# Attention with a rotation and mixing layer: an order from a longest-chain plan, weights turned by DMA, fp16 mixing halves

## The chip, the cores and the metric

One core of one Trainium2 chip. The metric is the device time of one execution in microseconds (us), lower is better. The kernel runs on TensorE (PE in the profile, PEld for its weight loads), VectorE (DVE), ScalarE (ACT), GpSimd (POOL) and SyncE (SP), whose queue issues all the DMAs here.

## What is computed

Eight batches of eight heads of causal attention over 576 positions with a window of 128 and a slope per head, then a layer over the 512 channels of each batch. Cut to what matters:

```python
scores = q @ k.T / sqrt(64) - slope[h] * (t - s)        # where 0 <= t - s < 128, else -1e9
attn = softmax(scores);  x[b] = concat over heads of attn @ v   # 576 x 512
theta = x @ w_theta
zr, zi = x * cos(theta), x * sin(theta)
y = w_tok_r @ zr + w_tok_i @ zi                         # mixes the 576 positions
u = x + y
out = u + maximum(u @ w_ch, 0)
```

The weights come in as 64-bit floats, whose words the kernel takes apart itself. All products are made from two halves of each operand (a high part and the rest), in three products out of four.

## The kernel before, in words

Work is done by pairs of heads (32 pairs, four to a batch). For a pair, q and k are loaded (L176, L178) and split into halves on ACT, DVE and POOL (L230 to L234). `Pair.scores` multiplies them (L289: six products a tile and pair of heads, five tiles), DVE adds the mask and takes the minimum of each row (L296), and ACT makes the exponentials (L300). `Head.turned` turns the weights on PE, nine transposes a head, into a PSUM tile `t_ps` (L320). Batch 0 ("early" heads) copies that out in fp32 (L356). From batch 1 on ("late" heads) `flip` writes two fp16 halves from PSUM into `pt`: the high one on ACT (L366), the low one on DVE (L367). `values` multiplies them with fp16 halves of v (L337: 27 matmuls a late head), and `finish` divides (L343 to L346) into `x_sb`, of which there is one buffer.

When a batch is whole, `turn` transposes x (L390), splits it (L401, L402), multiplies with w_theta (L410: 12 matmuls of 512 columns a column block), makes sine and cosine (L421 to L432; they need another table of ACT than the exponentials, hence the ACT_TABLE_LOADs) and writes z = x cos, x sin as two fp32r halves `z_hi`, `z_lo` (L434 to L440, L381 on ACT, L382 on POOL). `mix` is the big product with the token weights: 8 groups of 27 matmuls of 288 columns a batch, all operands fp32r (L469), then u and its halves (L474 to L476). `channels` is 8 groups of 12 matmuls (L489), a DVE step (L492) and the store (L494).

The order: Python generators interleave the mixing of batch b with the attention of batch b+1 (`attend`), and the channels of b with the turn of b+1 (`rotated`); priorities (MIX, CHAN, ROTATE) are hints to the language's scheduler, which sets the final order of each engine. While batch 0's attention runs, `unpack` takes the weights apart in 17 jobs (L127 to L150), mostly on DVE and POOL.

Of the kernel before, what the change touches and what calls it, by code (L numbers as in the profile page):

```python
# [11 lines left out]
F32 = mybir.dt.float32  # L12
# [4 lines left out]
BF16 = mybir.dt.bfloat16  # L17
# [26 lines left out]


@with_exitstack
def attn_moe_kernel(ctx: ExitStack, tc: tile.TileContext, qt, kt, vx, wth, wtok, wch, band, out):
    nc = tc.nc
    PSUM = bass.MemoryType.PSUM

    const = ctx.enter_context(tc.tile_pool(name="const", bufs=1))
    ld = ctx.enter_context(tc.tile_pool(name="ld", bufs=1))
    qk = ctx.enter_context(tc.tile_pool(name="qk", bufs=1))
    vp = ctx.enter_context(tc.tile_pool(name="vp", bufs=2))
    vbp = ctx.enter_context(tc.tile_pool(name="vbp", bufs=2))
    sp = ctx.enter_context(tc.tile_pool(name="sp", bufs=6))
    ptp = ctx.enter_context(tc.tile_pool(name="ptp", bufs=4))
    xp = ctx.enter_context(tc.tile_pool(name="xp", bufs=1))
    xtp = ctx.enter_context(tc.tile_pool(name="xtp", bufs=2))
    tp = ctx.enter_context(tc.tile_pool(name="tp", bufs=2))  # L60
    uf = ctx.enter_context(tc.tile_pool(name="uf", bufs=2))
    big = ctx.enter_context(tc.tile_pool(name="big", bufs=1))
    ps_s = ctx.enter_context(tc.tile_pool(name="ps_s", bufs=1, space=PSUM))
    ps_t = ctx.enter_context(tc.tile_pool(name="ps_t", bufs=2, space=PSUM))
    ps_a = ctx.enter_context(tc.tile_pool(name="ps_a", bufs=1, space=PSUM))
    ps_m = ctx.enter_context(tc.tile_pool(name="ps_m", bufs=3, space=PSUM))

    class Ring:


        def __init__(self, at, width, count):
            self.at, self.width, self.count, self.n = at, width, count, 0

        def take(self):
            c = self.at + self.n % self.count * self.width
            self.n += 1
            return fixed[:, c:c + self.width]

# [12 lines left out]
    nc.sync.dma_start(out=bnd, in_=band)
    nc.vector.memset(ones, 1.0)

    for g in range(H // 2):
        for e in range(2):
            nc.vector.memset(scales[64 * e:64 * e + 64, g:g + 1], -0.125 * 2.0 ** (2 * g + e + 1))

    wth_hi = const.tile([128, 4, DM], F32R, name="wth_hi")
    wth_lo = const.tile([128, 4, DM], F32R, name="wth_lo")
    wch_hi = const.tile([128, 4, DM], F32R, name="wch_hi")  # L100
    wch_lo = const.tile([128, 4, DM], F32R, name="wch_lo")
    wtk_hi = const.tile([128, 9, S], F32R, name="wtk_hi")
    wtk_lo = const.tile([128, 9, S], F32R, name="wtk_lo")

    nc.vector.memset(rebias, -float(916 << 23))

    ORDER = (0, 4, 1, 5, 2, 6, 3, 7, 8)

    def unpack(jobs, places):

        def load(k):
            src, hi, lo, c, w, scale = jobs[k]
            pool, name = places[k % len(places)]
            t = pool.tile([128, 4 * S], I32, name=name)
            nc.sync.dma_start(out=t[:, :2 * w], in_=src[:, c, :].bitcast(I32))
            return t

        def words(k, t):  # L120
            w = jobs[k][4]
            raw = t[:, :2 * w].rearrange("p (n t) -> p n t", t=2)
            return raw, t[:, 2 * S:2 * S + w], t[:, 3 * S:3 * S + w]

        def apart(k, t):
            raw, ex, ma = words(k, t)
            nc.vector.tensor_scalar(out=ex, in0=raw[:, :, 1], scalar1=0x7FF00000, scalar2=None,  # L127
                                    op0=ALU.bitwise_and)
            nc.vector.tensor_scalar(out=ma, in0=raw[:, :, 1], scalar1=0xFFFFF, scalar2=0x100000,
                                    op0=ALU.bitwise_and, op1=ALU.bitwise_or)  # L130
            nc.scalar.activation(ex, ex, AF.Relu, bias=rebias, scale=8.0)

        def together(k, t):
            raw, ex, ma = words(k, t)
            val = ma.bitcast(F32)
            nc.vector.scalar_tensor_tensor(out=ex, in0=raw[:, :, 1], scalar=-0x80000000, in1=ex,
                                           op0=ALU.bitwise_and, op1=ALU.bitwise_or)
            nc.vector.scalar_tensor_tensor(out=val, in0=raw[:, :, 0].bitcast(U32), scalar=2.0 ** -32, in1=ma,
                                           op0=ALU.mult, op1=ALU.add)
            nc.gpsimd.tensor_tensor(out=val, in0=val, in1=ex.bitcast(F32), op=ALU.mult)  # L140

        def split(k, t):
            _, hi, lo, c, w, scale = jobs[k]
            val = words(k, t)[2].bitcast(F32)
            if scale is None:
                nc.scalar.copy(hi[:, c, :], val)
                nc.gpsimd.tensor_tensor(out=lo[:, c, :], in0=val, in1=hi[:, c, :].bitcast(F32), op=ALU.subtract)
            else:
                nc.scalar.activation(hi[:, c, :], val, AF.Copy, scale=scale)
                nc.vector.scalar_tensor_tensor(out=lo[:, c, :], in0=val, scalar=scale, in1=hi[:, c, :].bitcast(F32),  # L150
                                               op0=ALU.mult, op1=ALU.subtract)

        tiles = {}
        n = len(jobs)
        for k in range(n + 3):
            for stage, fn in ((3, split), (2, together), (1, apart)):
                j = k - stage
                if 0 <= j < n:
                    if j not in tiles:
                        tiles[j] = load(j)  # L160
                    fn(j, tiles[j])
                    if stage == 3:
                        del tiles[j]
                    yield
            if k < n and len(tiles) < len(places):
                tiles[k] = load(k)

    JOBS = ([(wth, wth_hi, wth_lo, c, DM, TURN) for c in range(4)]
            + [(wtok, wtk_hi, wtk_lo, c, S, None) for c in ORDER])
    LATE = [(wch, wch_hi, wch_lo, c, DM, None) for c in range(4)]  # L170


    def load_pair(p):
# [538 lines left out]
```

## Time and profile before

| | |
|---|---|
| time, median of 3 runs | 796.17 us (796.0 to 796.47) |
| span of the profiled execution | 794.3 us, 1.9 us under that median; the page gives no other time for it |
| PE busy / PEld busy | 735.4 us (93%) / 651.7 us (82%) |
| DVE / ACT / POOL busy | 570.5 (72%) / 481.5 (61%) / 259.2 us (33%) |
| moved by DMA | 49.65 MB, mean 62 GB/s |
| clock granted to TensorE | 1.000 throughout |

All numbers below are of core 0, in us from the start of the span. "Busy" of PE is the time covered by matmuls from start to modelled end, so pipelined matmuls cover each other; what a matmul costs is read from the distance of the starts, or from a run of many in the chain of waits. A "DVE busy" of a window is covered time too.

### The profile page before, as it was taken

The numbers are of one execution on the slowest core, as the hardware profiler recorded it, in microseconds if no ns is written. First come the engines' busy times: TensorE is split into PE (matmuls) and PEld (weight loads), VectorE is DVE, ScalarE is ACT, GpSimd is POOL, SyncE is SP. The second block draws the span as 40 slices with busy tenths as digits, with TensorE's granted clock in tenths as the row PEclk, the third lists the DMA queues.
The fourth block names the chain that finished last, engine by engine and source line by source line (L and its number), as shares of the span: only waits on it lengthen the run. The fifth ranks groups of instructions, "written<-read, shape, count | busy, mean of one in ns | idle before, by whom it ended". The sixth has DMA issues, their size and how long they took to land.

```text
span 794.3 us, 16395 instructions
## 1 busy us (share of the span) xinstructions
PE 735.4 (93%) x6338; PEld 651.7 (82%) x6338; DVE 570.5 (72%) x1535; ACT 481.5 (61%) x962; POOL 259.2 (33%) x324
## 2 busy tenths in 40 slices
PE   3655799899999999999999999999999999999998
PEld 2444687789788898989888988999898988899897
DVE  5999847888767887687767777778767776654712
ACT  5445447776477656775668557855677666844610
POOL 3577511532143213332243215321423215210530
PEclk9999999999999999999999999999999999999999
DMA  6453211122202211022212211112102221000001
GB/s 239 153 173 108 65 44 50 31 65 64 84 30 72 65 46 53 24 64 68 80 38 65 65 45 61 52 60 80 53 24 65 65 74 48 2 1 32 31 1 60
DMA packets 29549, 49.65 MB, mean 62 GB/s; under 512 B 2592, under 2 KB 19104, under 8 KB 29472
## 3 DMA queue, kind: packets, MB, share of 16 engines
q1 hardware_dynamic: 29472, 48.61, 19.4%
q8 instruction: 50, 0.82, 0.4%
q14 instruction: 27, 0.22, 0.1%
HBM read 39.16 MB, written 9.44 MB: 61 GB/s over the span
## 4 chain that ended last, share of the span: by engine, by line
PE 62%; DVE 15%; ACT 15%; issue 4%; DMA 2%; POOL 1%; SPq 0%; DVEq 0%; ACTq 0%; POOLq 0%
PE mm L469 20%; PE mm L489 10%; PE t_ps L320 8%; PE mm L410 8%; PE s_ps L289 7%; PE acc L337 7%; ACT s_sb L300 6%; DVE f L425 2%; ACT g L431 2%; ACT z_hi L381 2%; DVE s_sb L296 2%; PE mm L390 2%; DVE g L427 1%; ACT L300 1%; ACT L431 1%
## 5 line engine op out<-in xcount | busy, mean ns | idle before, releaser
L469 PE MATMUL mm<-wtk_hi,z_hi 128*128 128x288 f32 x576 | 172.1, 304 | 3.0 <-ACT z_hi L381 1.7
L469 PE MATMUL mm<-wtk_lo,z_hi 128*128 128x288 f32 x576 | 171.2, 301 | 0.0
L469 PE MATMUL mm<-wtk_hi,z_lo 128*128 128x288 f32 x576 | 166.3, 299 | 0.5 <-POOL z_lo L382 0.5
L300 ACT ACTIVATE s_sb<-s_sb,fixed 128x256 f32<-128x256 f32 (+2 forms) x320 | 128.3, 465 | 54.6 <-DVE fixed L296 54.6
L296 DVE CUSTOM_DVE_ANT_0 s_sb<-s_ps,fixed 128x256 f32<-128x256 f32 (+2 forms) x320 | 105.3, 374 | 21.4 <-PE t_ps L320 11.3
L469 PEld LDWEIGHTS mm<-wtk_hi,z_hi 128*128 128x128 f32 x576 | 107.6, 188 | 6.6 <-ACT z_hi L381 2.1
L320 PE MATMUL t_ps<-fixed,s_sb 128*128 128x128 f32 (+1 forms) x576 | 103.1, 294 | 10.1 <-ACT s_sb L300 9.6
L469 PEld LDWEIGHTS mm<-wtk_lo,z_hi 128*128 128x128 f32 x576 | 108.0, 189 | 1.9
L469 PEld LDWEIGHTS mm<-wtk_hi,z_lo 128*128 128x128 f32 x576 | 106.2, 188 | 1.9 <-POOL z_lo L382 0.7
L476 POOL TENSOR_TENSOR u_lo<-xtf,u_hi 128x288 fp32r<-128x288 f32 x64 | 52.1, 822 | 138.4 <-ACT u_hi L475 125.8
L382 POOL TENSOR_TENSOR z_lo<-g,z_hi 128x512 fp32r<-128x512 f32 x40 | 54.6, 1365 | 126.2 <-ACT z_hi L381 126.2
L367 DVE SCALAR_TENSOR_TENSOR pt<-t_ps,pt 128x512 f16<-128x512 f32 x112 | 74.8, 683 | 23.6 <-ACT pt L366 23.6
L320 PEld LDWEIGHTS t_ps<-fixed,s_sb 128*128 128x128 f32 (+1 forms) x576 | 67.2, 150 | 27.2 <-ACT s_sb L300 14.5
L366 ACT ACTIVATE pt<-t_ps 128x512 f16<-128x512 f32 x112 | 63.5, 594 | 24.8 <-PE t_ps L320 24.3
L289 PE MATMUL s_ps<-kh,qh 64*128 64x256 f32 (+2 forms) x320 | 57.0, 341 | 21.9 <-DVE fixed L296 14.8
L234 POOL TENSOR_TENSOR kl<-kr,kh 128x576 fp32r<-128x576 f32 x32 | 46.6, 1457 | 71.9 <-ACT kh L233 62.4
L337 PE MATMUL acc<-vh,pt 128*128 128x65 f16 x1008 | 61.5, 195 | 2.7 <-DVE pt L367 1.7
L289 PEld LDWEIGHTS s_ps<-kh,qh 64*128 64x128 f32 (+1 forms) x320 | 32.8, 190 | 36.9 <-DVE fixed L296 14.9
L337 PEld LDWEIGHTS <-pt 128*128 128x128 f16 x1512 | 52.7, 98 | 10.0 <-DVE pt L367 2.6
L337 PE MATMUL acc<-vl,pt 128*128 128x64 f16 x504 | 55.9, 193 | 0.0
L475 ACT CAST u_hi<-xtf 128x288 fp32r<-128x288 f32 x64 | 27.2, 429 | 46.6 <-DVE xtf L474 46.6
L289 PE MATMUL s_ps<-kh,ql 64*128 64x256 f32 (+2 forms) x320 | 50.4, 300 | 5.0 <-DVE ql L231 5.0
(115 smaller groups left out, 1568.2 us busy)
## 6 DMA issues: line engine op xcount, KB each, us to landing
vb<-in_vx_dram SPq DMA_DIRECT2D x16, 650.0 KB, 4.3
qr<-in_qt_dram SPq DMA_DIRECT2D x32, 288.0 KB, 3.1
kr<-in_kt_dram SPq DMA_DIRECT2D x32, 288.0 KB, 2.8
out_dram<-xtf SPq DMA_DIRECT2D x64, 144.0 KB, 1.8
xtf<-in_wtok_dram SPq DMA_DIRECT2D x4, 576.0 KB, 4.9
u_hi<-in_wtok_dram SPq DMA_DIRECT2D x3, 576.0 KB, 3.8
u_lo<-in_wtok_dram SPq DMA_DIRECT2D x2, 576.0 KB, 3.9
xtf<-in_wth_dram SPq DMA_DIRECT2D x2, 512.0 KB, 9.4
```

Of the source, the lines that this page charges most:

```text
L289: nc.tensor.matmul(ps[:qn, e, 256 * k:256 * k + kn], qm[rows, q0:q0 + qn], km[rows, k0:k0 + kn], start=(j == 0), stop=(j == len(self.terms ...
L296: nc.vector.tensor_tensor_reduce(out=sb, in0=ps[:qn, e, 256 * k:256 * k + kn], in1=bnd[:qn, c0:c0 + kn], scale=2.0 ** -((2 * self.p + e) % ...
L300: self.exp = nc.scalar.activation(sb, sb, AF.Exp, bias=least, scale=-1.0)
L320: nc.tensor.transpose(t_ps[:, off:off + w], self.sc[i][:, 128 * j:128 * j + 128], ident[:w, :w])
L337: nc.tensor.matmul(av[:, i, :r.shape[-1]], l, r, start=(n == 0), stop=(n == len(prods) - 1))
L366: nc.scalar.activation(pt[:, 0], t_ps, AF.Copy, scale=2.0 ** PEXP)
L367: nc.vector.scalar_tensor_tensor(out=pt[:, 1], in0=t_ps, scalar=2.0 ** PEXP, in1=pt[:, 0], op0=ALU.mult, op1=ALU.subtract)
L382: nc.gpsimd.tensor_tensor(out=z_lo[:, c, :], in0=z, in1=z_hi[:, c, :].bitcast(F32), op=ALU.subtract)
L410: nc.tensor.matmul(t_ps, a[:, c * 128:c * 128 + 128], w[:, c, :], start=(k == 0 and c == 0), stop=(k == len(prods) - 1 and c == 3))
L469: nc.tensor.matmul(y_ps[:, :HALF], z[:, c, m * 128:m * 128 + 128], w[:, c, cs], start=(k == 0), stop=(k == 26))
L476: nc.gpsimd.tensor_tensor(out=u_lo[:, m, cs], in0=xtf[:, m, cs], in1=u_hi[:, m, cs].bitcast(F32), op=ALU.subtract)
L489: nc.tensor.matmul(o_ps[:, :HALF], w[:, c, e * 128:e * 128 + 128], u[:, c, cs], start=(k == 0), stop=(k == 11))
```

## The change

Nearly every line of the program is rewritten, the arithmetic is mostly the same. By parts:

1. **The order.** Each step (a run of instructions on one engine) is entered in a `Plan` with an assumed cost, an engine, and what it reads and writes; `Buf` and `Ring` derive who must wait for whom, buffers included. `Plan.order` gives each step a rank, its longest chain of costs to the end, and then plays the five engines forward, each taking the open step of highest rank (ACT holds its table unless another step is ahead by HOLD). The instructions are issued in that order and not moved any more.
2. **Late weights turned by DMA.** The exponentials of a group of tiles (groups (0, 2), (3, 4) and (1), both heads) are split in SBUF into fp16 halves `hl`, the high one by one ACT instruction (L491), the low one by one DVE instruction (L493) of 1024 or 256 elements a partition; a transposing DMA on SP's queue (L496) then writes `pt`. The late PE transposes and the copies out of PSUM are gone. Batch 0 is as before.
3. **Mixing in fp16.** z and the token weights are kept as fp16 halves. For that the token weights are brought to a common scale (a sum over the exponents' words on PE, a maximum on DVE; scaled once more on ACT) and z is multiplied by a scale of its batch (L639, now scalar_tensor_tensor in place of tensor_tensor; `z_scale` adds five one-column DVE instructions a batch), taken off again in the step after the mixing (L698). The mixing goes in runs of nine matmuls (L692).
4. **Buffers.** Two x buffers, two xtf, two accumulators `a_ps`; the halves have places of their own, and PSUM is split by use (one double bank for scores, two each for `a_ps`, `t_ps`, `m_ps`). Mixing and channels share the two `m_ps`.

The core of the diff:

```diff
+class Plan:
+    def __call__(self, engine, cost, emit, r=(), w=(), table=None):
...
+    def order(self):
+        steps = self.steps
+        for s in reversed(steps):
+            s.rank = s.busy + s.late + max((steps[a].rank for a in s.after), default=0.0)
...
+                if e == "ACT":
+                    best = min(open_[e], key=lambda x: (x[0] + (HOLD if steps[x[1]].table not in (None, table)
+                                                                else 0.0), x[1]))
...
-        def flip(self, bank):
-            t_ps, places = self.turned(bank)
-            pt = ptp.tile([128, 2, 512], F16, name="pt")
-            nc.scalar.activation(pt[:, 0], t_ps, AF.Copy, scale=2.0 ** PEXP)
-            nc.vector.scalar_tensor_tensor(out=pt[:, 1], in0=t_ps, scalar=2.0 ** PEXP, in1=pt[:, 0],
-                                           op0=ALU.mult, op1=ALU.subtract)
...
+            plan("ACT", act(2 * width), lambda hl=hl, sb=sb: nc.scalar.activation(
+                hl.tile[:, :, 0], sb.tile, AF.Copy, scale=2.0 ** PEXP), r=whole_sb, w=[(hl, "h")])
+            plan("DVE", dve(2 * width, True), lambda hl=hl, sb=sb: nc.vector.scalar_tensor_tensor(
+                out=hl.tile[:, :, 1], in0=sb.tile, scalar=2.0 ** PEXP, in1=hl.tile[:, :, 0], op0=ALU.mult,
+                op1=ALU.subtract), r=whole_sb + [(hl, "h")], w=[(hl, "l")])
+            plan("SP", (2.4, 2.6) if wide else (1.3, 1.5), lambda hl=hl, ptv=ptv: nc.sync.dma_start_transpose(
+                out=ptv, in_=hl.tile.rearrange("p e a k -> p (e a k)")), r=[(hl, "h"), (hl, "l")], w=[(pt, 0)])
...
-    wtk_hi = const.tile([128, 9, S], F32R, name="wtk_hi")
-    wtk_lo = const.tile([128, 9, S], F32R, name="wtk_lo")
+    wtk_hi, wtk_lo = place("wtk_hi", [128, 9, S], F16), place("wtk_lo", [128, 9, S], F16)
+    z_hi, z_lo = place("z_hi", [128, 9, DM], F16), place("z_lo", [128, 9, DM], F16)
...
-                nc.vector.tensor_tensor(out=xtf[:, m, cs], in0=y_ps[:, :HALF], in1=xtf[:, m, cs], op=ALU.add)
+                plan("DVE", dve(HALF), lambda y=y, at=at: nc.vector.scalar_tensor_tensor(
+                    out=at, in0=y.tile[:, :HALF], scalar=zs.tile[:, 1:2], in1=at, op0=ALU.mult, op1=ALU.add),
...
+    with tc.manual_schedule():
+        plan.run()
```

What the change moves, at three places.

First PE, where the mixing of batch 0 begins. Before, the names `mm` are the shared PSUM tiles of turn and mixing, `s_ps` the scores:

```order
L289 MATMUL s_ps<-kl,qh 128x256 x2
L289 MATMUL s_ps<-kh,qh 128x256 x2
L289 MATMUL s_ps<-kh,ql 128x256 x2
L289 MATMUL s_ps<-kl,qh 128x256 x2
L410 MATMUL mm<-wth_hi,x_hi 128x512 x4
L410 MATMUL mm<-wth_lo,x_hi 128x512 x4
L469 MATMUL mm<-wtk_hi,z_hi 128x288
L469 MATMUL mm<-wtk_lo,z_hi 128x288
L469 MATMUL mm<-wtk_hi,z_lo 128x288
```

After (PE again, the 35th and 36th matmul of the mixing and what follows; `t_ps` here holds the small products that measure v, `a_ps` the values' accumulator, `pta` the turned weights):

```order
L692 LDWEIGHTS z_lo
L692 MATMUL m_psb<-wtk_hi,z_lo 128x288
L417 MATMUL t_psb<-fixed 128x4
L408 MATMUL t_psa<-fixed 4x128
L459 MATMUL s_ps<-kh,qh 128x128 x2
L459 MATMUL s_ps<-kh,ql 128x128 x2
L459 MATMUL s_ps<-kl,qh 128x128 x2
L417 MATMUL t_psb<-fixed 128x4
L563 LDWEIGHTS pta
L563 MATMUL a_psa<-vha,pta 128x65
```

Before, the mixing follows the turn of batch 0 at once, with 174 score matmuls (5.8 pairs) and half a pair of late values ahead of it. After, 36 of its matmuls stand there, with 192 score matmuls ahead of the first; then come the values of all four pairs of batch 1 and scores up to 270 matmuls (9 pairs), and then the rest.

Second ACT, in the middle of the program, where it goes from sine to exponentials. Before (`f`, `g` are the angles, `s_sb` the weights):

```order
L424 ACTIVATE g<-f 64x512
L431 ACTIVATE g<-g,fixed 64x512
L432 ACTIVATE f<-f 64x512
L300 ACT_TABLE_LOAD
L300 ACTIVATE s_sb_4995<-s_sb_4995,fixed 64x192
L300 ACTIVATE s_sb_4996<-s_sb_4996,fixed 64x192
L300 ACTIVATE s_sb_4995<-s_sb_4995,fixed 128x256
```

After, ACT at such a place (`fgb` holds the angles, `sbc` and `sba` the weights, `hln` the fp16 halves of tile 1):

```order
L491 ACTIVATE hlna<-sbna 128x2x128
L633 ACT_TABLE_LOAD
L633 ACTIVATE fgb<-fgb,fixed 128x512
L635 ACTIVATE fgb<-fgb 128x512
L589 CAST xpb<-t_psb 128x4x64
L598 COPY xtfb<-t_psb 128x4x64
L644 CAST z_hi<-fgb 128x512
L477 ACT_TABLE_LOAD
L477 ACTIVATE sbc<-sbc,fixed 128x256
L644 CAST z_hi<-fgb 128x512
L477 ACTIVATE sbc<-sbc,fixed 128x256
```

The sines of a batch no longer stand together: exponentials come between them, with a table load each way. The whole program has 54 table loads after and 16 before.

Third SP, whose queue now also issues the transposing DMAs. Before, in the middle of the program:

```order
L192 DMA vb<-in_vx_dram 128x4x325
L178 DMA kr<-in_kt_dram 128x576
L176 DMA qr<-in_qt_dram 128x576
L494 DMA out_dram<-xtf 128x288 x3
L178 DMA kr<-in_kt_dram 128x576
L176 DMA qr<-in_qt_dram 128x576
L494 DMA out_dram<-xtf 128x288 x5
```

After, SP in the middle (`pta` to `ptd` and `ptn` are written by a transposing DMA):

```order
L496 DMA_TRANSPOSE pta<-hla 128x16x128
L496 DMA_TRANSPOSE ptb<-hlb 128x16x128
L496 DMA_TRANSPOSE ptna<-hlna 128x4x128
L395 DMA vba<-in_vx_dram 128x4x325
L730 DMA out_dram<-xtfa 128x288 x6
L496 DMA_TRANSPOSE ptc<-hla 128x16x128
L496 DMA_TRANSPOSE ptd<-hlb 128x16x128
L374 DMA kra<-in_kt_dram 128x576
L372 DMA qra<-in_qt_dram 128x576
```

Three transposing DMAs a pair, 84 in all, stand in one queue with the loads and the stores; the loads and stores behind one in the queue wait for its halves to be ready.

More of the change, by code (lines that the diff above doesn't have):

```diff
@@ L59, in attn_moe_kernel @@
[L59 to L66, printed above, removed]
@@ L153, in unpack @@
[L153 to L166, printed above, removed]
@@ new lines, in whole, with keep @@
+        return finish
+    def keep(c, w, val, ex, E, M):
+        plan("POOL", pool(w), lambda: nc.gpsimd.tensor_tensor(out=held[c].tile, in0=val, in1=ex, op=ALU.mult),
+             r=[E, M], w=[(held[c], 0)])
+    for c in range(4):
+        unpack(wth, c, DM, whole(wth_hi, wth_lo, theta_w, TURN))
+    for k, c in enumerate(ORDER):
+        unpack(wtok, c, S, keep, first=k == 0, last=k == 8, summed=True)
+    ws_buf = Buf()
+    for k in range(2):
+        plan("DVE", dve(HALF), lambda k=k: nc.vector.tensor_reduce(
+            out=peak[:, k:k + 1], in_=sums[k].tile[:, :HALF], axis=mybir.AxisListType.X, op=ALU.max),
+            r=[(sums[k], 0)], w=[(ws_buf, k)])
@@ L373, in turn, with turned @@
-    def turn(x_sb, st):
-        xtf = uf.tile([128, 4, S], F32, name="xtf")
-        z_hi = big.tile([128, 9, DM], F32R, name="z_hi")
-        z_lo = big.tile([128, 9, DM], F32R, name="z_lo")
-        st.update(xtf=xtf, z_hi=z_hi, z_lo=z_lo)
-        def split_z(c, z):
-            nc.scalar.copy(z_hi[:, c, :], z)
-            nc.gpsimd.tensor_tensor(out=z_lo[:, c, :], in0=z, in1=z_hi[:, c, :].bitcast(F32), op=ALU.subtract)
+            def turned(t_ps=t_ps, jobs=jobs):
+                for off, w, src in jobs:
+                    nc.tensor.transpose(t_ps.tile[:, off:off + w], src, ident[:w, :w])
@@ new lines, in early_head, with multiply @@
+            plan("PE", pe(115 * len(jobs)), turned, r=read, w=[(t_ps, 0)])
+            plan("ACT", act(512), lambda t_ps=t_ps, bank=bank: nc.scalar.copy(
+                pt.tile[:, 512 * bank:512 * bank + 512], t_ps.tile), r=[(t_ps, 0)], w=[(pt, bank)])
+        acc = a_ring.take()
+        av = acc.tile[:, :NT * 65].rearrange("p (i d) -> p i d", d=65)
+        def multiply():
+            for i in range(NT):
+                for j, c in enumerate(CHUNKS[i]):
+                    nc.tensor.matmul(av[:, i, :], parts[i][j], vb.tile[:, k, c, :], start=(j == 0),
+                                     stop=(j == len(CHUNKS[i]) - 1))
@@ L384, in columns, with turn @@
+    def turn(x_buf, zs):
+        xtf = xtf_ring.take()
+        every = [(x_buf, h) for h in range(H)]
+        ahead = {}
         def columns(i):
@@ L443, in turn @@
[L443 to L461 removed]
+                plan("ACT", act(256), lambda: nc.scalar.copy(both[:, :, 0], src), r=[(x_ps, 0)], w=[(xp, "h")])
@@ L462, in mix @@
+    def mix(xtf, zs):
         for hf in range(2):
+            cs = slice(hf * HALF, hf * HALF + HALF)
             for m in range(4):
[L464 to L473 removed]
@@ L650, in attn_moe_kernel @@
[L650 to L664 removed]
+                o = m_ring.take()
@@ new lines, in attn_moe_kernel @@
+    last = None
+    for b in range(B):
+        x_buf = x_ring.take()
+        for g in range(EARLY):
+            p = b * EARLY + g
+            if p <= EARLY:
+                ready(p)
+            if p >= EARLY:
+                ready(p + 1)
+            for e in range(2):
+                head = early_head if b == 0 else late_head
+                head(2 * p + e, pair_weights[p][e], x_buf)
+            pair_weights.pop(p)
+        if last is not None:
+            mix(last[1], last[2])
+            channels(last[0], last[1])
+        zs = z_scale(b)
+        last = b, turn(x_buf, zs), zs
```

988 lines of the change are left out of this document (536 added, 452 removed).

## Prediction

> **What bounds the kernel now.** I read the page first: the engines' shares and the slices.
>
> ```profile
> span 794.3 us, 16395 instructions
> PE 735.4 (93%) x6338; PEld 651.7 (82%) x6338; DVE 570.5 (72%) x1535; ACT 481.5 (61%) x962; POOL 259.2 (33%) x324
> PE   3655799899999999999999999999999999999998
> DVE  5999847888767887687767777778767776654712
> PE 62%; DVE 15%; ACT 15%; issue 4%; DMA 2%; POOL 1%; SPq 0%; DVEq 0%; ACTq 0%; POOLq 0%
> ```
>
> Two regimes are to be seen: a start of about eight slices in which DVE is full and PE is not, and then PE at 9 to the end. The windows give each its size: the start up to the first exponentials after the turn of batch 0, one slice of the start, one batch of the middle, and the end.
>
> ```profile
> core 0: us, PE busy (x) PEld busy (x) DVE busy (x) ACT busy (x) POOL busy (x), PEclk, DMA share, GB/s
> 0.00:155.83 155.83, 108.09 (x602) 87.75 (x603) 124.83 (x290) 84.39 (x159) 73.77 (x68) 1.00 0.34 110
> 40.00:80.00 40.00, 21.97 (x107) 18.45 (x107) 39.42 (x65) 20.57 (x39) 28.98 (x23) 1.00 0.43 139
> 417.24:504.01 86.77, 86.21 (x805) 77.06 (x804) 64.62 (x188) 58.06 (x117) 26.25 (x37) 1.00 0.19 58
> 746.85:794.34 47.49, 43.72 (x325) 42.95 (x324) 13.01 (x25) 8.23 (x17) 10.20 (x11) 1.00 0.09 32
> ```
>
> Each batch of the middle takes 86.8 us, and PE is covered for 86.2 of them. But cover is not cost. The costliest group of the page, and four of its matmuls in the timeline:
>
> ```profile
> L469 PE MATMUL mm<-wtk_hi,z_hi 128*128 128x288 f32 x576 | 172.1, 304 | 3.0 <-ACT z_hi L381 1.7
> ...
> 411.58 0.29 PE L469 MATMUL mm<-wtk_hi,z_hi 128*128 128x288 f32 x1
> 411.71 0.29 PE L469 MATMUL mm<-wtk_lo,z_hi 128*128 128x288 f32 x1
> 411.84 0.30 PE L469 MATMUL mm<-wtk_hi,z_lo 128*128 128x288 f32 x1
> ```
>
> A mixing matmul lasts 300 ns and the next one starts 130 ns after it. So the three L469 groups like this one (some 516 us by their busy column) are 1728 x 0.13, about 230 us, of PE, and halving the width of the operands cannot free what the column shows. The costs come from runs in the chain of waits (start, us, what):
>
> ```profile
> 447.02 0.93 PE acc L337 x27
> 466.09 1.02 PE mm L390 x8
> 469.11 1.18 PE t_ps L320 x9
> 470.29 0.91 PE s_ps L289 x12
> 740.81 2.73 PE mm L410 x12
> 759.53 15.55 PE mm L469 x115
> 784.08 4.67 PE mm L489 x34
> ```
>
> That is per matmul 0.0344 (values), 0.1275 (x turned), 0.131 (weights turned), 0.076 (scores), 0.2275 (theta), 0.135 (mixing), 0.137 us (channels). A batch has 216 x 0.0344 = 7.4, 20 x 0.1275 = 2.6, 72 x 0.131 = 9.4, 120 x 0.076 = 9.1, 56 x 0.2275 = 12.7, 216 x 0.135 = 29.2 and 96 x 0.137 = 13.2: together 83.6 of the 86.77 us. PE is the bound of the middle, at 96%.
>
> **PE after the change.** The 72 late transposes of a batch go: -9.4. The mixing in fp16: no row shows a 288-column fp16 matmul. From above, it gains nothing (0.135). From below, the 512 columns of theta cost 0.2275, so 288 columns cost 0.128 if only the columns count; the values (fp16 weights, 65 columns, 0.034) show that fp16 weight loads are no limit at that rate. I take 0.128, since the value row excludes the weight load as the bound: 27.6, a gain of 1.6. The batch is then 72.6. At the same 96.3% it takes 75.4 us, 11.4 less than now.
>
> **What then is next.** DVE loses 16 low halves from PSUM and gets 8 wide (1024 elements) and 4 narrow ones (256) between SBUF operands.
>
> ```profile
> L367 DVE SCALAR_TENSOR_TENSOR pt<-t_ps,pt 128x512 f16<-128x512 f32 x112 | 74.8, 683 | 23.6 <-ACT pt L366 23.6
> ...
> L425 DVE SCALAR_TENSOR_TENSOR f<-f,mm x32: 673/687/690, 127.8 to 744.6; 128x512 f32<-128x512 f32 x32
> L425 DVE SCALAR_TENSOR_TENSOR f<-g,f x8: 683/1658/1840, 151.3 to 750.1; 64x512 f32<-64x512 f32 x8
> ...
> 412.35 1.29 POOL L382 TENSOR_TENSOR z_lo<-f,z_hi 128x512 fp32r<-128x512 f32 x1
> ...
> 412.53 1.66 DVE L425 SCALAR_TENSOR_TENSOR f<-g,f 64x512 f32<-64x512 f32 x1 [0.29 <-ACT g L424]
> ```
>
> The minimum, median and maximum of L425 tell both ends: with a PSUM operand it never takes more than 690 ns, with SBUF operands alone 683 when undisturbed and 1658 beside a POOL instruction. So a wide half costs 1.29 us (twice 0.683 less one start of 0.08, my estimate) and up to 0.97 more when it meets POOL, which is busy 26.25 of 86.77 us. Per batch: -16 x 0.683 = -10.9; 8 x 1.29 + 4 x 0.38 = +11.8; 12 meetings at 30% x 0.97 = +3.5 (0 to 11.6); the one-column steps of the scale +0.5. DVE goes from 64.6 to 69.5. The steps that become scalar_tensor_tensor keep their operands; for them I take nothing (they met POOL before as well; were all ten a batch to meet it anew, at 0.97, DVE would pass PE by 6.6).
>
> ACT loses 16 x 0.594 and gets 8 x 1.1 + 4 x 0.38 for the high halves (1.1: twice the 594 less a start). And it gets table loads: 54 against 16, over about seven batches 5.4 more in each.
>
> ```profile
> L366 ACT ACTIVATE pt<-t_ps 128x512 f16<-128x512 f32 x112 | 63.5, 594 | 24.8 <-PE t_ps L320 24.3
> L431 ACT ACT_TABLE_LOAD x8 | 10.3, 1283 | 0.1
> L300 ACT ACT_TABLE_LOAD x7 | 9.0, 1283 | 0.1
> ...
> 415.31 0.62 ACT L432 ACTIVATE f<-f 64x512 f32<-64x512 f32 x1
> 415.94 1.28 ACT L300 ACT_TABLE_LOAD   x1
> 417.24 1.20 ACT L300 ACTIVATE s_sb<-s_sb,fixed 64x192 f32<-64x192 f32 x3
> ```
>
> 5.4 x 1.283 = 6.9, so ACT goes from 58.1 to 65.8. The load at 415.94 stands 0.01 us behind the sine before it and 0.02 ahead of the exponential: the trace shows nothing around the 1.283.
> The Trainium skill (ScalarE: Activation LUTs, What ACT_TABLE_LOAD costs) puts a switch at 2.66 us, a drain of 1.38 on top; the trace does not show that drain.
>
> So after the change a batch asks 72.6 of PE, 69.5 of DVE and 65.8 of ACT: PE stays the bound by a little, and three engines stand close together in a fixed order.
>
> **The start.** DVE has 124.83 us of work up to 155.83. The order shows that 3.2 more pairs of scores and the values of four pairs are done before the mixing runs in earnest, all DVE work.
>
> ```profile
> L296 DVE CUSTOM_DVE_ANT_0 s_sb<-s_ps,fixed 128x256 f32<-128x256 f32 (+2 forms) x320 | 105.3, 374 | 21.4 <-PE t_ps L320 11.3
> ...
> L231 DVE SCALAR_TENSOR_TENSOR ql<-qr,fixed,qh 128x576 fp32r<-128x576 f32 x32 | 36.1, 1129 | 5.8 <-ACT qh L230 5.4
> L250 DVE SCALAR_TENSOR_TENSOR vl<-vb,fixed,vh 128x320 f16<-128x320 f32 x56 | 33.1, 592 | 13.7 <-ACT vh L248 13.6
> L346 DVE TENSOR_TENSOR x_sb<-acc,fixed 128x320 f32<-128x320 f32 x64 | 31.1, 486 | 1.0
> ```
>
> 32 x 0.374 = 12.0, 3 x 1.13 = 3.4, 8 x (0.59 + 0.49) = 8.6, five pairs of low halves at 2 x 1.29 + 0.38 = 14.8: +39, so about 163 us of DVE. At the 80% of the whole start today this is 204 us, at the 98.5% of the slice 40 to 80 it is 165. I take 93%, nearer to the slice, because attention of a second batch now lies beside the unpacking: 175 us.
>
> **The sum.** What is left for PE then: 8 mixings (220.8, less the 36 matmuls done, 4.6), 8 channels (105.6), 7 thetas and x (107.1), 6 batches of values (44.4), 690 scores (52.4): 525.7. Of these the last mixing and channels, 40.8, stand alone at the end, with the 3.8 us of gaps that today's end has (47.49 - 43.72). So 175 + (525.7 - 40.8)/0.963 + 44.6 = 723 us of span. The median lies 1.9 over the span: **725 us**. The bounds: the start at 165 or 204 gives 715 or 754, PE at 99% or 90% of the middle (490 or 539) 711 or 760, fp16 at 0.135 737; the two good ends together 701, the two bad ones 790, which is where the second rival begins.
>
> **Where the transposes go.** 84 transposing DMAs take them over, none of which the trace shows. Nearest are loads of like size (512 KB read and as much written for a wide one):
>
> ```profile
> xtf<-in_wtok_dram SPq DMA_DIRECT2D x4, 576.0 KB, 4.9
> ...
> xtf<-in_wth_dram SPq DMA_DIRECT2D x2, 512.0 KB, 9.4
> ```
>
> 4.9 us to landing, 9.4 with four loads queued. Two wide and a narrow (a quarter) are 2.25 wide ones a pair; a pair has 75.4/4 = 18.9 us, so one queue hides them up to 8.4 us each. I take 5, the row without a crowd, and no cost; pt has places for two pairs, which covers the latency.
>
> **The rivals.**
> *The transposes are slow, and it ends slower.* If a wide one holds the queue for 12 us, a pair takes 27 us, 28 pairs 756, and with about 160 us before the first and after the last (the start's four pairs, the last turn, mixing and channels) 916. It is slower than 796 from (796 - 160)/28/2.25 = 10.1 us on. For it: a transposing write is scattered, and loads behind it wait. Against: the row of 4.9. 0.07.
> The Trainium skill (VectorE: DVE Perf Modes, The three transpose paths) gives 1309 ns for one block of 128 x 128 by DMA against 390 on TensorE; by it, if blocks do not overlap, a wide one of 16 blocks is 20.9 us, a pair 47 and the whole about 1480, an estimate; no run here shows it.
> *The fixed order stalls.* Three engines at 96, 92 and 87% of a batch, each issuing in line: a late DVE step (a POOL meeting of 0.97) holds up ACT, that the transposing DMA, that PE's values and the mixing behind them. At 86% of PE and a start at 80% the sum is 204 + 564 + 45 + 2 = 815; at 88% and 190 it is 788. 0.13.
> *The start hides.* If mixing and the attention ahead overlap fully, DVE alone bounds all but the end: 570.5 - 76.5 (112 x 0.683) + 83 (28 pairs) + 25 (meetings) + 4 = 606, less 13 in the end, at 98% plus 45: 650; at 95% 669. Against: the values of batch 1 stand ahead of the rest of the mixing in the order. 0.17.
> *Table switches cost more than the load.* With a drain of about the load's own length around each, ACT has 7.4 x 1.28 = 9.5 more a batch, 75.3, and passes PE; at 96.3% 78.2 a batch, 2.8 x 6.7 = +19: 744. Against: the gaps of 0.01 and 0.02. 0.03. By the page's 1.38 it would be 749.
>
> **How the numbers follow.** The forecast (700 to 765) has 0.60 and its time is the prediction. The range 672 to 790 takes in the forecast, the table rival, over half of "the start hides" and half of the stalls: 0.8. Less than 0.2% is what a measurement of this kernel cannot tell from no change (its three runs differ by 0.06%). Faster: 0.60 + 0.17 + 0.03 + 0.08 of the stalls = 0.88; same 0.02; slower 0.10.
>
> **What would show it.** Right: mixing starts 0.128 us apart; PE covered over 95% in the middle at some 75 us a batch; transposing DMAs landing in about 5 us and no wait of the values on them; bulk mixing from about 175. Wrong: PE idle in the middle behind the values' accumulator (transposes late) or behind z (ACT, DVE), a start over 200, a batch over 82 us, or no gaps at all and mixing in earnest before 150.

## The result and the profile after

The changed kernel takes **745.42 us** (median of 4 runs, 742.7 to 746.52) where the kernel before took 796.32 (796.0 to 797.01, 4 runs beside it): ratio 0.9356, 95% interval 0.9336 to 0.9375. The profiled execution took 742.7 with a span of 740.9. 725 was forecast, 2.7% too low; the range held it.

From its page: the span, the busy times, the slices of PE, DVE and the granted clock, and the chain of waits by engine.

```profile
span 740.9 us, 15619 instructions
PE 644.9 (87%) x5876; PEld 535.3 (72%) x5876; DVE 595.9 (80%) x1565; ACT 539.7 (73%) x981; POOL 275.4 (37%) x266
PE   0989972847998989899999799979998899899998
DVE  7884999799889986998889988898789878935412
PEclk9985886767999999999999999999999999999999
PE 35%; DVE 28%; ACT 6%; issue 4%; POOL 1%; DMA 1%; SPq 0%; DVEq 0%; ACTq 0%; POOLq 0%
```

PE is no longer full from slice 8 on, its row has 8s and 7s, and DVE's share of the chain has gone from 15% to 28%. The windows below give the start (up to the mixing in earnest), three middle batches, each from its first theta matmul to the next batch's, and the end.

```profile
core 0: us, PE busy (x) PEld busy (x) DVE busy (x) ACT busy (x) POOL busy (x), PEclk, DMA share, GB/s
0.00:178.00 178.00, 119.10 (x863) 96.91 (x864) 148.40 (x403) 126.09 (x229) 72.06 (x69) 0.78 0.48 137
...
346.30:424.70 78.40, 72.73 (x733) 60.32 (x731) 70.10 (x188) 63.49 (x118) 29.36 (x29) 1.00 0.56 128
424.70:503.80 79.10, 72.75 (x732) 60.32 (x730) 69.61 (x182) 65.55 (x118) 30.68 (x29) 1.00 0.54 120
503.80:581.80 78.00, 73.06 (x731) 60.36 (x730) 68.00 (x188) 68.65 (x121) 29.24 (x29) 1.00 0.54 124
698.29:740.90 42.61, 39.33 (x312) 33.80 (x311) 8.12 (x17) 3.57 (x9) 7.99 (x10) 0.99 0.10 36
```

A batch takes 78.5 us (mean of the three) in place of 86.8. By stages the span changes so: the start from 155.8 to 178.0 (+22.2), the middle from 591.0 to 520.3 (-70.7), the end from 47.5 to 42.6 (-4.9): together -53.4, and 794.3 - 53.4 = 740.9.

Where the mixing begins, from the view of its line between 137 and 178 us (ns min/median/max, first and last start):

```profile
L692 PE MATMUL m_psa<-wtk_hi,z_hi x4: 286/286/429, 137.7 to 177.9; 128*128 128x288 f16 x4
...
L692 PE MATMUL m_psb<-wtk_lo,z_hi x3: 286/286/286, 138.9 to 139.7; 128*128 128x288 f16 x3
```

36 matmuls start between 134.4 and 139.8 us, and then none before 177.9. What one costs is read from the starts, here near the end:

```profile
699.75 0.29 PE L692 MATMUL m_psb<-wtk_hi,z_hi 128*128 128x288 f16 x1
699.88 0.29 PE L692 MATMUL m_psb<-wtk_lo,z_hi 128*128 128x288 f16 x1
700.00 0.29 PE L692 MATMUL m_psb<-wtk_hi,z_lo 128*128 128x288 f16 x1
700.12 0.29 PE L692 MATMUL m_psb<-wtk_hi,z_hi 128*128 128x288 f16 x1
```

Three intervals take 0.37 us, 0.123 each (0.128 was taken, 0.135 before). The Trainium skill (TensorE: Matmul & The Clock Gate, Part 2, Back-to-back issue gap) gives N/2.4 + 2.5 ns at full clock for the gap between two isolated matmuls of N columns, by which 288 columns would take 122.5 (an estimate), and the trace agrees. The transposing DMAs land in about the 5 us that were taken:

```profile
pta<-hla SPq DMA_TRANSPOSE x14, 4.7
ptb<-hlb SPq DMA_TRANSPOSE x14, 4.8
...
ptna<-hlna SPq DMA_TRANSPOSE x14, 2.9
```

**A correction to what stands above the prediction.** The clock of the kernel before was not 1.000 throughout. The clock row of its page says so, but the clock record of that trace begins only at 123 us, and its score matmuls show another clock up to about 118 us (ns min/median/max, first and last start):

```profile
L289 PE MATMUL s_ps<-kh,ql x14: 412/412/419, 98.6 to 117.7; 64*128 64x256 f32 x10, 64*64 64x192 f32 x2, 64*128 64x128 f32 x2
...
L289 PE MATMUL s_ps<-kh,ql x10: 272/278/299, 138.1 to 148.7; 64*128 64x256 f32 x6, 64*128 64x128 f32 x2, 64*64 64x192 f32 x2
```

The same instruction lasts 412 ns there and 278 later. In the changed kernel, whose record begins at 30 us, the same matmuls of 256 columns take 412 to 417 ns at a granted 0.5 and 274 to 281 at 1.0. So both starts run partly at half clock; only the middle of before was rightly at full speed.

### The profile page after: what moved, and what is told of

The parts are those of the page before. It is cut to its first block, busy times and chain, and to the rows that moved or that the text cites. A ratio compares the mean times of both kernels' runs of the same rounds, so it can differ in the third digit from the quotient of the medians.

```text
span 740.9 us, 15619 instructions
## 1 busy us (share of the span) xinstructions
PE 644.9 (87%) x5876; PEld 535.3 (72%) x5876; DVE 595.9 (80%) x1565; ACT 539.7 (73%) x981; POOL 275.4 (37%) x266
## 4 chain that ended last, share of the span: by engine, by line
PE 35%; DVE 28%; ACT 6%; issue 4%; POOL 1%; DMA 1%; SPq 0%; DVEq 0%; ACTq 0%; POOLq 0%
PE m_psa L692 10%; PE m_psb L692 10%; PE t_psa L613 6%; PE s_ps L459 3%; DVE fga L639 3%; DVE fgb L639 3%; PE m_psa L720 2%; DVE ql L384 2%; PE m_psb L720 2%; DVE hla L493 2%; DVE hlb L493 2%; DVE vlb L435 2%; DVE vla L435 1%; DVE sba L472 1%; DVE x_sba L513 1%
## 5 line engine op out<-in xcount | busy, mean ns | idle before, releaser
L692 PEld LDWEIGHTS <-z_hi 128*128 128x128 f16 x1152 | 108.1, 98 | 44.2 <-issue 15.3
L692 PE MATMUL m_psa<-wtk_hi,z_hi 128*128 128x288 f16 x288 | 83.3, 289 | 6.9 <-DVE xtfb L727 2.3
L692 PE MATMUL m_psb<-wtk_hi,z_hi 128*128 128x288 f16 x288 | 82.4, 286 | 4.2 <-DVE xtfb L698 1.9
L388 POOL TENSOR_TENSOR kl<-kra,kh 128x576 fp32r<-128x576 f32 x32 | 51.0, 1594 | 93.5 <-ACT kh L387 90.9
L692 PE MATMUL m_psa<-wtk_lo,z_hi 128*128 128x288 f16 x288 | 82.8, 288 | 0.0
L692 PE MATMUL m_psa<-wtk_hi,z_lo 128*128 128x288 f16 x288 | 82.7, 287 | 0.0
L692 PE MATMUL m_psb<-wtk_hi,z_lo 128*128 128x288 f16 x288 | 82.4, 286 | 0.0
L692 PE MATMUL m_psb<-wtk_lo,z_hi 128*128 128x288 f16 x288 | 82.4, 286 | 0.0
L645 POOL TENSOR_TENSOR z_lo<-fgb,z_hi 128x512 f16<-128x512 f32 x36 | 49.1, 1379 | 69.3 <-ACT z_hi L644 69.3
L692 PEld LDWEIGHTS <-z_lo 128*128 128x128 f16 x576 | 56.5, 98 | 14.4
L384 DVE SCALAR_TENSOR_TENSOR ql<-qra,fixed,qh 128x576 fp32r<-128x576 f32 x32 | 43.6, 1362 | 5.6 <-ACT qh L383 5.4
```

What stands on the lines that cost most here:

```text
L384: plan("DVE", dve(S, True), lambda: nc.vector.scalar_tensor_tensor(out=ql, in0=qr.tile, scalar=sc, in1=qh.bitcast(F32), op0=ALU.mult, op1= ...
L388: plan("POOL", pool(S), lambda: nc.gpsimd.tensor_tensor(out=kl, in0=kr.tile, in1=kh.bitcast(F32), op=ALU.subtract), r=[(kr, 0), (buf, "kh" ...
L645: plan("POOL", pool(512), lambda: nc.gpsimd.tensor_tensor(out=z_lo[:, c, :], in0=z, in1=z_hi[:, c, :], op=ALU.subtract), r=key + [(z_buf, ...
L692: nc.tensor.matmul(y.tile[:, :HALF], z[:, c, m * 128:m * 128 + 128], w[:, c, cs], start=(part == 0 and j == 0 and a == 0), stop=(part == 2 ...
```

## The experiments

Twelve kernels; the kernel before, run beside them, took 795.4 to 795.9 us. Each starts from the changed kernel unless said otherwise. Ratios are to the kernel before.

| run | us (range) | ratio, 95% interval |
|---|---|---|
| before, fp16 mixing alone | 777.6 (775.49 to 778.96) | 0.9773 (0.9756 to 0.979) |
| weights turned by PE again | 835.18 (833.64 to 836.13) | 1.0497 (1.0482 to 1.0513) |
| one x tile | 747.87 (747.12 to 750.21) | 0.9407 (0.9389 to 0.9424) |
| order by the language's scheduler | 861.86 (859.92 to 862.08) | 1.0836 (1.0817 to 1.0854) |
| each transposing DMA twice | 864.58 (859.66 to 868.4) | 1.086 (1.0818 to 1.0902) |
| the same into spare tiles, one x tile | 793.1 (790.27 to 796.94) | 0.9965 (0.995 to 0.998) |
| POOL's steps cut short | 708.34 (700.63 to 709.98) | 0.8881 (0.8833 to 0.893) |
| before, POOL's steps cut short | 787.15 (786.68 to 787.43) | 0.9889 (0.9876 to 0.9903) |
| idle matmuls in the start | 740.32 (739.2 to 741.74) | 0.9303 (0.9289 to 0.9317) |
| measured costs in the planner | 735.39 (726.25 to 737.86) | 0.9202 (0.914 to 0.9264) |
| both of these | 730.76 (726.21 to 731.37) | 0.9159 (0.9132 to 0.9185) |
| both, and patience at tables | 725.68 (724.89 to 726.53) | 0.9118 (0.9106 to 0.913) |

**Parts of the change one at a time.** The fp16 halves alone, put into the kernel before (without the common scale, so its small values lose precision):

```diff
-    wtk_hi = const.tile([128, 9, S], F32R, name="wtk_hi")
+    wtk_hi = const.tile([128, 9, S], F16, name="wtk_hi")
...
-        z_hi = big.tile([128, 9, DM], F32R, name="z_hi")
+        z_hi = big.tile([128, 9, DM], F16, name="z_hi")
```

> The kernel before with the third part alone: token weights and z as fp16 halves, without the common scales, so the low halves lose bits. Theory: a mixing matmul goes from 0.131-0.135 to 0.1225 us, 1728 times: 15 to 21 us less, 775 to 781, the middle still PE's at 96%. Rival (DVE, ACT and the waits between them set the batch, PE is only covered): no change, 793 to 797. Rival (the busy column is the cost, and half the width halves it): under 700.

777.6, as expected: in the kernel before, the mixing's type alone is worth 18 us, where the whole change gains 51. The DMA part undone, the rest kept:

```diff
...
-            plan("SP", (2.4, 2.6) if wide else (1.3, 1.5), lambda hl=hl, ptv=ptv: nc.sync.dma_start_transpose(
...
+                    nc.tensor.transpose(t_ps.tile[:, off:off + w], src, ident[:w, :w])
...
```

> The changed kernel with its second part undone: the late weights are turned on PE again (nine transposes a head into the m banks) and split out of PSUM by ACT and DVE; five places for the weights in place of three, everything else and the plan's rules as in the changed kernel. Theory (the middle is bound by PE, and the transposes were its largest saving): PE's demand a batch goes from 71.5 to 80.9 us, at 91 to 93% that is 87 to 89 us a batch in place of 78.4, over six to seven batches +55 to +70: 800 to 815 us. Rival (the order and the buffers made the gain, the transposes were hidden beside other work): under 765.

835.18: the rival fell, and the theory was 20 us short as well. Its middle batches:

```profile
299.20:395.20 96.00, 86.85 (x803) 70.84 (x803) 65.84 (x192) 65.45 (x123) 23.08 (x25) 0.93 0.17 52
395.20:489.40 94.20, 87.08 (x815) 71.72 (x815) 67.86 (x193) 61.87 (x121) 23.59 (x25) 0.96 0.18 55
489.40:588.90 99.50, 88.58 (x802) 70.98 (x802) 70.37 (x192) 62.47 (x121) 23.56 (x25) 0.91 0.16 50
```

PE is covered 14.7 us longer a batch than in the changed kernel, of which 9.4 are the transposes at the price that the kernel before shows. The other 5 go with the granted clock, which is down to 0.91 to 0.96; a further 3 us is idle. What makes the clock fall here and not in the kernel before, which also turned on PE, was not tried; there PE was covered 99% of a batch, here 91%.

The second x tile taken away:

```diff
-    x_ring = Ring(x_tiles, [[], held[8].users])
+    x_ring = Ring(x_tiles[:1], [[]])
```

> The changed kernel with one x buffer. Theory: the last step of a head must then wait until the turn of the batch before has read x for the last time, so the values come in a burst after the turn, with two accumulators to hold them: 2 to 6 us a batch, 757 to 785. Rival (the plan finds another order as good): 742 to 749.

747.87: the rival was right, the tile is worth 2 us. And the plan's steps written out in the order in which they are entered, for the language's scheduler to place:

```diff
-    with tc.manual_schedule():
-        plan.run()
+    for s in plan.steps:
+        s.emit()
```

> The changed kernel without the plan's order: the same steps issued in the order in which they are entered (pair by pair, then mixing and channels of the batch before, then the turn), and the language's scheduler orders the engines, as in the kernel before. Theory (parts two and three cut PE's work by 11 us a batch, the plan only makes that usable, at 92%): with a worse order 760 to 800. Rival (the plan's order is itself the gain): 800 or more. Rival (the order is worth nothing): 745.

861.86, slower than before and in the rival's range (800 or more): without its own order the rewritten kernel loses 116 us. The theory had given the order less than half of that. The granted clock is lower too, 0.87 in the mean of the span for 0.94; how much of the 116 us comes by way of it was not separated.

**Have the transposes room?** Each transposing DMA twice in a row, to the same place:

```diff
-            plan("SP", ..., lambda hl=hl, ptv=ptv: nc.sync.dma_start_transpose(
-                out=ptv, in_=...), ...
+            plan("SP", ..., lambda hl=hl, ptv=ptv: [nc.sync.dma_start_transpose(
+                out=ptv, in_=...) for _ in range(2)], ...
```

> Every transposing DMA is issued twice in a row, the second one writing the same values again; the order of every engine stays that of the changed kernel. Theory (the transposes are hidden, the queue has slack): landings of 4.4 to 4.8 us for a wide one leave a pair at 2.25 x 4.6 = 10 us of a period's quarter of 19.6; doubled it would still be 21 us if landings did not overlap, but they overlap, so the time stays at 745 to 752. Rival (the queue is close to its limit, and a part of the missing 20 us of my forecast is transposes that come late): each pair takes at least 21 us, 1.1 to 1.5 more than now, over 28 pairs 30 to 45 us more: 775 to 790. In between would mean that only the latency, 4 us more for each pair's last weights, is felt in places.

864.58: both were wrong, the theory by far. The waits of SP's queue and of PE (us in total, times, longest; longer waits of the stores for DVE are left out, they stand in the changed kernel too):

```profile
SPq L496 <- DMA ptd<-hlb: 38.6, 14, 4.1
...
SPq L496 <- DMA ptc<-hla: 34.0, 14, 4.1
SPq L496 <- DMA pta<-hla: 33.0, 14, 4.0
```

```profile
PE a_psa L563 <- DMA ptnb<-hlna: 42.0, 7, 8.9
```

The second DMA waits for the first one's landing, and SP stands still meanwhile, 191 us over the six tiles, with the loads and the next transposes behind it. PE's values then wait for the narrow one, 9 us at the longest. To separate the standing still from the transfers, the second copy went into two spare tiles that nobody reads (in the room of the second x tile), so that it waits for nothing:

```diff
+    spares = ring("spare", 2, [128, 16, 128], F16)
...
+                nc.sync.dma_start_transpose(out=o, in_=hl.tile.rearrange("p e a k -> p (e a k)")) for o in (ptv, sp)], r=...
```

> Only one x tile, which took 747.9 us by itself, and in the room that this frees two spare tiles: each transposing DMA is issued a second time into a spare tile that nobody reads, so that, unlike the doubled run, the second does not wait for the first. Theory A (the doubled run lost 119 us because SP stood still for 2.5 to 4 us at each second DMA; the transfers themselves have room): 748 to 765. Theory B (the transfers of a wide one fill the queue for 4 to 5 us, so doubling them fills a pair's time whatever SP does): 830 to 870.

793.1, between the two: the second copies cost 45 us over the run with one x tile, and the larger part of the 119 of the other run goes with SP's standing still and with values that wait for the second landing. The 45 us are not the transfers' alone: SP needs 2.7 us more for each wide one to issue it, and ACT waits 18 us in all for second copies to release the halves that they read. The queue's row (packets, MB, share of 16 engines' span) of the run with one x tile, and with the second copies:

```profile
q1 hardware_dynamic: 161184, 81.65, 46.1%
```

```profile
q1 hardware_dynamic: 292896, 114.69, 69.6%
```

In the waits of PE the values stand behind the narrow one again:

```profile
PE a_psa L564 <- DMA ptnb<-hlna: 32.7, 7, 6.0
```

69.6% of 791.1 less 46.1% of 745.4 is 207 us for 63 wide ones (56 and 28 quarters): 3.3 us of all 16 engines each. So the transposes of one batch fill 30 of its 78 us on the DMA engines.

**What makes a batch 78 and not 75?** POOL's three large steps cut to an eighth of their columns after the first use (the low halves of z, u and k are left incomplete), at unchanged planned costs, so that the order of all engines stays:

```diff
+        n = 72 if p else S
         plan("POOL", pool(S), lambda: nc.gpsimd.tensor_tensor(
-            out=kl, in0=kr.tile, in1=kh.bitcast(F32), op=ALU.subtract), ...
+            out=kl[:, :n], in0=kr.tile[:, :n], in1=kh[:, :n].bitcast(F32), op=ALU.subtract), ...
```

> Three of POOL's steps (low halves of z, of u and of k) compute only an eighth of their columns after their first use, so their result is left out for the rest; nothing else changes, the order of all engines is that of the changed kernel. Theory A (the three engines miss each other in a fixed order because DVE's steps that meet POOL are longer than planned): with POOL at about 70 us of short work DVE loses 3 to 5 us a batch and PE's share of a middle batch rises from 91% towards 96%: 720 to 730. Theory B (the losses are elsewhere: order, table loads, clock): 740 to 746.

708.34: theory A, and 12 us beyond it. What PE waited for in the changed kernel from 269 to 582 us, four batches (us in total, times, longest):

```profile
PE s_ps L459 <- DVE fixed L472: 7.8, 7, 2.2
PE t_psb L583 <- DVE xpb L595: 1.9, 2, 1.1
PE m_psb L692 <- DVE xtfb L698: 1.9, 1, 1.9
```

So it goes on: all of the 22.8 us that PE is idle there end with a step of DVE, none with POOL, ACT or a DMA. With POOL cut short 6.2 us of such waits are left over four batches. In the changed kernel POOL and DVE meet like this (timeline of the low halves of k and of q, and all 32 of q in ns min/median/max):

```profile
432.92 1.88 POOL L388 TENSOR_TENSOR kl<-kra,kh 128x576 fp32r<-128x576 f32 x1 [11.18 <-ACT kh L387]
...
433.56 1.86 DVE L384 SCALAR_TENSOR_TENSOR ql<-qra,fixed,qh 128x576 fp32r<-128x576 f32 x1
...
L384 DVE SCALAR_TENSOR_TENSOR ql<-qra,fixed,qh x32: 796/1457/1955, 16.1 to 613.3; 128x576 fp32r<-128x576 f32 x32
```

The groups of the page (busy, mean ns, idle before) add what it comes to and that PE hardly waits for POOL's halves of k either:

```profile
L384 DVE SCALAR_TENSOR_TENSOR ql<-qra,fixed,qh 128x576 fp32r<-128x576 f32 x32 | 43.6, 1362 | 5.6 <-ACT qh L383 5.4
...
L459 PE MATMUL s_ps<-kl,qh 64*128 64x256 f32 (+2 forms) x320 | 45.9, 283 | 0.8 <-POOL kl L388 0.8
```

With POOL cut short, the same step:

```profile
L385 DVE SCALAR_TENSOR_TENSOR ql<-qra,fixed,qh x32: 796/818/1708, 16.1 to 581.8; 128x576 fp32r<-128x576 f32 x32
```

and two of its batches:

```profile
327.70:402.20 74.50, 72.55 (x732) 60.29 (x730) 62.00 (x188) 62.72 (x118) 13.85 (x29) 1.00 0.59 130
402.20:475.50 73.30, 72.02 (x733) 60.21 (x730) 61.28 (x182) 64.78 (x118) 13.40 (x29) 1.00 0.60 129
```

The median of ql falls from 1457 to 818 ns, DVE from 69 to 62 us a batch, the batch to 73.7 (mean of four), and PE is covered for 98% of it. It is the meeting that costs, not the length of POOL's own work: PE's matmuls with kl waited 0.8 us for POOL in the whole changed kernel. Of the 7.3 us of DVE a batch (mean of four) the low halves of q account for 2.1, those of v for 1.9, the products with sine and cosine for 1.5 and the new halves for 1.1.

The same cut in the kernel before:

> The kernel before the change with the same three POOL steps cut to an eighth of their columns after their first use (their result is left out for the rest). In the changed kernel this cut saved 37 us. Theory (a DVE step made long by POOL costs time only where DVE is nearly as busy as TensorE; in the kernel before TensorE bounds the middle at 99% covered and DVE has 22 us a batch to spare): only the start gains, 785 to 796. Rival (the meetings cost time in any kernel, through waits on DVE's results): 755 to 775.

787.15, a gain of 8.7 in place of 37 (here the shortened low halves are kept in one tile each, and the scheduler may shift the order a little, since the costs change). A stretch of its middle:

```profile
417.00:504.00 87.00, 87.00 (x814) 78.14 (x813) 63.10 (x189) 59.03 (x121) 8.90 (x37) 1.00 0.20 58
```

PE is covered all of it. The four batches from the third theta to the seventh take 346.1 us where they took 346.0, and DVE is busy for 61.9 us a batch where it was 64.5. So there the meetings cost DVE 2.6 us a batch, and the middle did not wait for them; the gain lies ahead of these batches and behind them. In the changed kernel the meetings cost 7.3, and PE waits.

Next, eight planned costs set to what the changed kernel's trace measured, for instance

```diff
-        plan("DVE", dve(S, True), lambda: nc.vector.scalar_tensor_tensor(      # ql
+        plan("DVE", (1.25, 0.15), lambda: nc.vector.scalar_tensor_tensor(
```

> Eight costs in the planner are set to the durations measured in the changed kernel's trace (for instance 1.25 instead of 0.6 us for the low half of q); the planner then makes another order. Theory A (the fixed order loses time because its planned durations are wrong by up to a factor of two): 725 to 738. Theory B (the order is limited by the way the list is built, not by its costs; 68 table loads instead of 53 cost ACT 19 us): 743 to 765.

735.39: theory A. The batches of the new order:

```profile
352.30:428.00 75.70, 72.82 (x731) 60.21 (x731) 66.37 (x188) 68.16 (x121) 28.40 (x29) 1.00 0.56 129
428.00:503.60 75.60, 72.67 (x730) 60.11 (x730) 66.20 (x188) 68.16 (x121) 28.42 (x29) 1.00 0.59 128
```

75.6 us with POOL's work whole: the order made for the measured durations wins back most of the 3 us that were missing, although ACT loads its table 68 times in place of 54 (and the start of this run is 6 us longer). Its four executions spread from 726 to 738 us, and the profile is of the longest. DVE is busy 66.3 us a batch in place of 69.2, and there the wide halves take 1.20 to 1.23 us each: in this order they miss POOL, which the planner knows nothing of. So part of the gain may be the luck of another order; that was not tested.

**The start.** Three idle matmuls ahead of each early transposing step:

```diff
             def turned(t_ps=t_ps, jobs=jobs):
+                for _ in range(3):
+                    nc.tensor.matmul(t_ps.tile[:, :128], white, ident, start=True, stop=True)
```

> Three idle matmuls of 128 fp32 columns are put ahead of each early transposing step on TensorE (their result is overwritten). Theory A (between 50 and 77 us and up to 179 the granted clock is 0.5 because TensorE's work there is too thin, and it costs about 10 us, since TensorE is covered 10 of 10 us there and DVE 4): the clock stays at 1.0 for more of the start, theta of batch 0 takes 8 instead of 15 us, bulk mixing starts 5 to 10 us earlier: 735 to 741. Theory B (the start is set by DVE, or the clock does not follow these matmuls): 745 to 750, the clock of the start as before.

740.32, theory A at its upper end, although the mixing in earnest begins only 3 us earlier (174.9 for 177.9) and not 5 to 10. The window of 50 to 77 us in the changed kernel:

```profile
50.00:77.00 27.00, 25.22 (x124) 23.21 (x125) 16.10 (x49) 10.79 (x23) 6.80 (x6) 0.50 0.26 88
```

and with the idle matmuls:

```profile
50.00:77.00 27.00, 24.40 (x204) 21.47 (x203) 22.91 (x67) 15.70 (x32) 9.80 (x11) 1.00 0.31 101
```

A group of early values in it (busy, mean ns), first in the changed kernel:

```profile
L546 PE MATMUL a_psa<-vbb,pta 128*128 128x65 f32 x18 | 4.1, 420 | 0.0
```

```profile
L548 PE MATMUL a_psa<-vbb,pta 128*128 128x65 f32 x18 | 2.2, 278 | 0.0
```

At half clock PE was the bound there (25 of 27 us covered, DVE 16). With more matmuls the clock stays at 1.00, 18 values take 2.2 in place of 4.1 us, and DVE comes to 22.9. Of these 6.8 us more of DVE's work 5 are left at the end.

**A version that beats both.** The measured costs and the idle matmuls together:

> Both at once: the eight measured costs in the planner and the three idle matmuls ahead of each early transposing step. Theory (they act at different places: the costs shorten a middle batch from 78.3 to 75.7 us, the idle matmuls the start by 4 us): 728 to 733. Rival (the new order has already changed the start, so that the idle matmuls no longer help there): 735 to 738.

730.76, as expected; the two add up (its five executions lie in two groups, 726.2 to 726.9 and 730.8 to 731.4). And the planner leaves ACT idle for up to 2 us before it changes its table:

```diff
-HOLD = 6.0
+HOLD = 60.0
+PATIENCE = 2.0
...
+                    if other.table not in (None, table) and table is not None and now < other.ready + PATIENCE - 1e-9:
+                        wake.append(other.ready + PATIENCE)
+                        continue
```

> As the run with both, and the planner leaves ACT idle for up to 2 us before it changes the function table, which brings the table loads down by about a quarter. Theory A (table loads, each 1.283 us, add to the delays although TensorE is covered 96% of the middle): 3 to 8 us less than the run with both. Theory B (ACT's time has slack, the waiting itself delays the weights): the same or up to 10 us more.

725.68: 5 us less in the median, though hardly less than the lower group above, with 56 loads for 68. The new order differs in more than that, so the 5 us are not shown to be the loads' alone. With the whole computation done, this is 20 us faster than the changed kernel and 70 than the kernel before.

## Why the prediction was right, and where its size was off

The direction and the mechanism held: PE gives up the transposes and a little of the mixing, and the middle becomes shorter. 18 us of the span were missing (723 against 740.9): start +3.0, middle +16.8, end -2.0. Some luck is in it: each mixing was 1.1 us cheaper than taken, which hid a part of the miss in the middle.

- **Mixing in fp16, the end, the overhead: right.** 0.123 us a matmul for 0.128, the end 42.6 for 44.6, 1.8 us around the span for 1.9. (The busy columns of the three mixing groups before add up to 509.6 us, not some 516; nothing hangs on it.)
- **The demand of the engines: right.** DVE 69.2 us a batch (mean of the three windows) for 69.5, ACT 65.9 for 65.8, PE, with 0.123 us a mixing matmul, 71.5 for 72.6. Table loads are 54 at 1283 ns, and the rival with a drain has nothing in the trace.
- **"At the same 96.3% it takes 75.4 us": the step that failed.** It carried over an efficiency from a kernel in which PE was alone at its limit to one in which three engines are busy for 93, 88 and 84% of the batch. The batch took 78.5, and by the same measure, demand over batch, PE came to 91%; it was covered for 93% of the batch where it had been for 99%. It is the mild form of the second rival, whose 86% was not reached, and by a shorter path: PE waited for DVE itself, not for values behind a late transposing DMA. The runs name the cause: steps of DVE that meet POOL take up to two and a half times their time alone (ql 1955 for 796 ns), at places where the fixed order has no slack. Without POOL's load a batch takes 73.7, with an order made for the measured durations 75.6.
- **"For them I take nothing": wrong.** The meetings of the new halves were put at 3.5 us a batch, the old steps at none. Cutting POOL takes 2.6 us of DVE a batch in the kernel before and 7.3 in the changed one. 4.7 are new, not far from the 3.5, but not where they were put: the meetings of the new halves cost 1.1, ql alone went from a mean of 1129 to 1362 ns, while the wide halves, taken at 1.29 us alone, had a mean of 1.34 with their meetings. That the sum of DVE came out right is luck: the new halves took 12.5 us a batch where 15.3 were forecast, and the other steps together some 2.5 more than taken.
- **The start: near, for two wrong reasons.** 175 was forecast as 163 us of DVE at 93%; it was 148.4 at 83%, in 178. The prediction took the clock for full, and the run with the idle matmuls, which lifts the clock in a part of the start, gains 5 us.
- **The transposes are hidden: right, but with less room than 8.4 us each.** No wait of the values on them showed. But that bound gave SP's queue to them alone. With each issued twice to the same place, SP spent 18.7 us a pair of heads on issuing them and standing still between the two, and 2.5 on loads and stores: 21.2 of the 24.2 us that a pair then took, where it had been 8.1 of 19.6. So the first rival's mechanism is real and a nearly full queue shows it at twice the length, though its sum with that figure, 28 x 21.2 + 160 = 754, does not reach the 864.6 measured: waits in the queue for other engines come on top, and not all of the rest is accounted for. Where SP did not stand still, the second copies still cost 45 us. The Trainium skill (VectorE: DVE Perf Modes, The three transpose paths) has 1309 ns for a block of 128 x 128; here the 16 blocks of a wide one land in 4.4 to 4.8 us and the 4 of a narrow one in 2.6 to 2.9, less than 0.2 us for each block more, so by the trace blocks are not paid one after the other.
- **Turning on PE: more than the 9.4 us a batch.** With the planner's rules kept it costs 18 a batch, as the run that undid it shows.

## What to carry to other kernels

An efficiency measured while one engine is alone at its limit did not carry over here, where the change brought three engines within 10% of each other: price the batch with the spread of each step's duration, not with its mean. A planner's fixed order depends on its durations; a new order from those read back in the trace of the planned kernel was worth 10 us here. A queue that hides one transfer should be asked what it does while it waits: second copies that the issuing engine had to wait for cost 119 us, those that it did not wait for 45.

## What the runs showed of the hardware

- The granted clock falls to 0.5 with TensorE covered 25.2 of 27 us, in a stretch of short fp32 matmuls and transposes; with 49 plain matmuls more it stayed at 1.00. The Trainium skill (TensorE: Matmul & The Clock Gate, Part 4: PE-mode transpose) says that transposes do not count as busy time there in the same way. The second of these numbers fits that, but transposes cover only 4.8 of the 25.2 us and plain matmuls of the values 15.7, so it does not by itself explain the 0.5, and what does is not shown.
- The clock row of a page can be wrong where its record begins late (here at 123 us); the duration of one repeated matmul (412 against 278 ns) tells the clock without it.
- A step of DVE that meets one of POOL can last more than twice as long: the low half of q takes 796 ns at the least, 1457 in the median and 1955 at the most beside POOL's full steps, and 818 in the median with these cut short.
- Sixteen transposed blocks cost 3.3 us of all 16 DMA engines, some 2090 packets, though only 0.5 MB are written.
